# Attention and a cosine feed-forward layer on one core: cosine without an absolute value, weights' range by row sums, the state times r in 64x32 parts of the array, x's columns in another order

## The chip, the cores and the metric

The program runs on one core of a Trainium2 chip. The metric is its device time in microseconds, the median of several runs; lower is better. A profile of one execution stands beside the times.

## The reference

Two stages. A linear attention with a state per head (batch 4, 8 heads, 768 positions, 48 channels a head), and a feed-forward layer on its output (3072 tokens of 384 channels, 2048 hidden):

```python
for t in range(S):
    cur = einsum('bhd,bhe->bhde', u * k[t], v[t])
    y[t] = einsum('bhd,bhde->bhe', r[t], state + cur)
    state = w[..., None] * state + einsum('bhd,bhe->bhde', k[t], v[t])
x = y.transpose(0, 2, 1, 3).reshape(B * S, H * D)
h = x @ w_in
out = (h * cos(h)) @ w_out
```

The feed-forward weights `moe_w_in` and `moe_w_out` arrive as 64-bit floats; the others as 32-bit floats.

## The kernel before

**A written order.** Every operation (some instructions of one engine) is given to a planner (`Plan`, L72) with an engine, a due time, a cost and a latency in microseconds, what it comes after, and the buffers that it uses. The planner runs through a simulated clock, always starts the operation that can start first (among equals the one with the earlier due time), and gives buffers out of rings. What comes out is the program order of each engine; at run time each engine works through its instructions in that order, and waits where an input isn't there. The steps of the feed-forward part are the unit of due times. "ACT" is ScalarE, "DVE" VectorE, "POOL" GpSimd, "PE" TensorE, "SP" the engine that issues most DMAs.

**Attention** (`chunk`, L577) works on 24 chunks: 128 positions of one batch, all 8 heads, in four pairs of heads. A chunk loads r, k and v, brings k and r into transposed, decayed form (kT, rT), and forms the 128x128 scores A of each head on PE (`mm_a`, L736, 48 rows of the array, even heads in rows 0 to 47 and odd ones in 64 to 111, each half into its own PSUM bank). ACT writes the diagonal (`diagonal`, L726) and DVE puts the scores above it (`mask`, L745). The chunk's x, 384 rows of 128 positions in one PSUM bank, is the sum of two products: `mm_x` (L755), state times rT, in 12 matmuls with 112 rows and 32 columns of the array; and `mm_x2` (L765), v times A, in 16 matmuls with 128 rows and 32 columns. For `mm_x` the state `zc` of a batch, whose heads lie in two blocks of partitions, is first spread by two ACT copies into a tile `zt` that is zero elsewhere (`spread`, L786). x leaves PSUM once on ACT in rounded form (`xh`, L823) and once on DVE as the remainder (`xl`, L828). `mm_z` (L791) and `state` (L835) bring the state forward. Chunks 0 to 11 ("early") come before the feed-forward part and share seven PSUM banks; chunks 12 to 23 ("late") are woven into it, have three banks, and load r and k in pieces of 32 rows that DVE transposes.

**Weights.** 32 slices (16 of w_in, 16 of w_out, 384 KB each) are loaded into one of two `raw` buffers as pairs of 32-bit words (`load_raw`, L419), and turned into a high and a low part by `conv` (L485): ACT L511, DVE L519 and L531, POOL L542 (after which `raw` is free), ACT L547, DVE L552. Later every slice is loaded again and `check_range` (L429) tests that each value lies in the range in which that conversion is right: one ACT and four DVE instructions of 384 columns (L432, L438, L447, L456, L465). If any test fails, a flag makes the program run a slower general path behind the main one.

**The feed-forward part** has 128 steps: a slice of 128 hidden units for a block of three chunks. `mm_h` (L222) is nine matmuls of 384 columns into one of two or three PSUM banks; then come, in turn on ACT and DVE, `whole` (L241, h/2pi rounded to a whole number), `rest` (L244), `size` (L247, the absolute value), `cosine` (L250), the product with h (L944), and its high and low part (L947, L950); `mm_o` (L233) is nine matmuls into three accumulators. Blocks 0 to 3 go through slices 0-1, 2-4, 5-9 and 10-15 in turn, so the slices are needed one after another: slice 2 at step 8, slice 5 at step 20, slice 10 at step 40. An accumulator leaves through ACT (L978) or DVE (L980) and is stored by SP, or added in memory by a DMA of POOL.

Of the kernel before, what the change touches and what calls it, by code (L numbers as in the profile page):

```python
# [163 lines left out]
def kernel(  # L164
# [42 lines left out]
    quarter = const.tile([P, 1], F32, name="quarter")  # L207
    nc.vector.memset(quarter, 0.5 * math.pi)
# [32 lines left out]
    def whole(qi, ph):  # L241
        nc.scalar.activation(qi, ph, AF.Copy, scale=INV_2PI)  # L242
# [4 lines left out]
    def size(q):  # L247
        nc.scalar.activation(q, q, AF.Abs)  # L248

    def cosine(q):  # L250
        nc.scalar.activation(q, q, AF.Sin, scale=-TWO_PI, bias=quarter)  # L251


    with ExitStack() as actx:
# [12 lines left out]
        R_r = ring("r", 2, [P, H, DP], F32)  # L267
# [10 lines left out]
        R_f = ring("f", 8, [P, DM], F32)  # L278
# [21 lines left out]
        fine_all = att.tile([P, 2 * NF + 3], F32, name="fine")  # L300
        fine = fine_all[:, 0 : 2 * NF]
        fine_p = fine_all[:, 2 * NF : 2 * NF + 1]
        fine_m, fine_w = (fine_all[0:1, 2 * NF + i : 2 * NF + i + 1] for i in (1, 2))
# [14 lines left out]
        def start_pool2():  # L318
            for t in R_zt:
                nc.gpsimd.memset(t.ap, 0.0)  # L320
# [29 lines left out]
        b_w = Buf(B_EARLY)  # L350
        o_wT = op(PE, -95, 0.1, lambda: nc.tensor.transpose(b_w()[:, 0:NP], wr.rearrange("p j d -> p (j d)"), ident[0:NP, 0:NP]), [o_w, o_wr, o_pool], [b_w], lat=0.3)
# [67 lines left out]
        def load_raw(i, raw):  # L419
            f, part = divmod(i, 2)  # L420
            if part == 0:
# [7 lines left out]
        def check_range(i, due, behind):  # L429
            raw, ca, cb = Buf(R_raw), Buf(R_f), Buf(R_f)  # L430
            o0 = op(SP, due - 3.0, 1.6, lambda: load_raw(i, raw), [behind], [raw], lat=3.4)
            o1 = op(ACT, due, 0.47, lambda: nc.scalar.activation(ca(), f32(raw()[:, :, 1]), AF.Abs), [o0], [raw, ca])  # L432

            o2 = op(
                DVE,
                due,
                0.5,
                lambda: nc.vector.scalar_tensor_tensor(ca(), ca(), 0.0, ca(), op0=ALU.is_equal, op1=ALU.add),  # L438
                [o1],
                [ca],  # L440
                port=True,
            )
            o3 = op(
                DVE,
                due,
                0.27,
                lambda: nc.vector.tensor_scalar(cb(), ca(), F64_TINY, F64_HUGE, op0=ALU.max, op1=ALU.min),  # L447
                [o2],
                [ca, cb],
                port=True,  # L450
            )
            o4 = op(
                DVE,
                due,
                0.5,
                lambda: nc.vector.tensor_tensor(cb(), cb(), ca(), op=ALU.is_equal),  # L456
                [o3],
                [ca, cb],
                port=True,
            )  # L460
# [3 lines left out]
                0.5,  # L464
                lambda: nc.vector.tensor_reduce(fine[:, i : i + 1], cb(), op=ALU.min, axis=AX.X),  # L465
                [o4],
                [cb],
# [4 lines left out]
        def fine_min():  # L472
            nc.vector.tensor_reduce(fine_p, fine, op=ALU.min, axis=AX.X)
# [11 lines left out]
        def conv(i, due, behind=None):  # L485
# [20 lines left out]
            o0 = op(SP, due - 3.5, 1.6, lambda: load_raw(i, raw), [behind], [raw], lat=3.4)  # L506
# [54 lines left out]

        last_A = [None]
        last_z = [None] * B
# [13 lines left out]
        def chunk(i, due, xbuf):  # L577
# [11 lines left out]
            xp = Buf(bk)  # L589
# [11 lines left out]
            if late:  # L601
                rb = Buf(R_f)
                ks, rs = Buf(R_raw), Buf(R_raw)

# [39 lines left out]
            l_r = op(SP, due - 5.1, 1.35, load_r, ahead, [rb], lat=2.6, line=ln)  # L644
# [10 lines left out]
            if late:  # L655
# [10 lines left out]
                t_k = op(DVE, due - 2.9, 0.71, tr_s(kT, ks), [l_ks], [ks, kT])  # L666
                e_k = op(POOL, due - 2.8, 1.4, decay_s(kT, decT_k), [t_k], [kT], port=True)
                t_r = op(DVE, due - 2.8, 0.71, tr_s(rT, rs), [l_rs], [rs, rT])
                e_r = op(POOL, due - 2.7, 1.4, decay_s(rT, decT_r), [t_r], [rT], port=True)
            else:  # L670
                t_r = op(PE, due - 2.4, 0.43, tr(rTp, rb), [l_r, o_pool], [rb, rTp, rT], lat=0.3)
# [16 lines left out]
                [rb, kb, mb],  # L688
# [45 lines left out]
            o_d = [op(ACT, due - 1.55 + 0.01 * j, 0.9, diagonal(j), [o_a, o_pool], [ab, A[j]], line="diagonal") for j in range(2)]  # L734
# [17 lines left out]
            def xv():  # L752
                return xp()[:, 0 : NK * C].rearrange("q (kk t) -> q kk t", kk=NK)

            def mm_x():  # L755
                x = xv()
                for g in range(NK * 4):
                    p, s = divmod(g, 3)
                    gs = slice(G * (g % 4), G * (g % 4) + G)
                    nc.tensor.matmul(  # L760
                        x[gs, g // 4, :], zb()[:, p, G * s : G * s + G], rT()[0:KP, p, :], start=(g < 4), stop=False,
# [3 lines left out]
            def mm_x2():  # L765
                x = xv()
                for g in range(NK * 4):
                    p, s = divmod(g, 3)
# [30 lines left out]
            def mm_xz():  # L799
                if c:  # L800
                    mm_x()
# [360 lines left out]
```

## Time and profile before

| | |
|---|---|
| median of 3 runs | 528.02 us (526.63 to 528.57) |
| the profiled execution | 527.78 us, of which the span of the instructions is 526.1 us |
| PE busy | 511.6 us (97% of the span) |
| DVE, ACT, POOL busy | 427.2, 394.9, 177.4 us |
| granted TensorE clock, mean | 0.997 |
| DMA | 61.60 MB, mean 117 GB/s |

Busy time is that in which an engine has an instruction under way. Matmuls overlap, so PE's is not a measure of its work: for that, one reads when matmuls start. A group's row gives line, engine, operation, what it writes from what, shape and number, then busy us and mean ns of one, then idle time of the engine before these instructions and what ended it. PEld is PE's loading of weights into the array. SPq rows are DMAs that SP issues.

### The profile page before, as it was taken

The page shows a single profiled execution, that of the slowest core. Times are in us where ns is not written, and L with a number is a line of the kernel's source. Part 1 is how long each engine was busy: PE and PEld are TensorE (multiplying, and loading weights), DVE is VectorE, ACT ScalarE, POOL GpSimd, SP SyncE. Part 2 cuts the span into 40 slices and gives each one's busy share as a digit, 9 for nine tenths or more (in the row PEclk, how much of TensorE's full clock was granted, in tenths as well). Part 3 has the DMA queues.
Part 4 walks back from the last instruction along what each step waited for, and adds up shares of the span by engine and source line. Part 5 has one row for each costly group of instructions (what it writes and reads, how often), then busy time and mean ns, then how long its engine had stood idle before and what let it go on. Part 6 is the DMA issues. An engine that isn't in the chain of part 4 may idle for free.

```text
span 526.1 us, 11829 instructions
## 1 busy us (share of the span) xinstructions
PE 511.6 (97%) x4428; PEld 482.2 (92%) x4428; DVE 427.2 (81%) x835; ACT 394.9 (75%) x933; POOL 177.4 (34%) x184
## 2 busy tenths in 40 slices
PE   8999999999999999999999999899999999999995
PEld 6787799999999999999999999898999999999994
DVE  5688788889888787566899999999889998886453
ACT  3888988988888777758687787586867877776664
POOL 6766423255354244224426224404043040400000
PEclk9999999999999999999999999999999999999998
DMA  9897235667846495414584853646356453500001
GB/s 140 142 167 154 58 115 184 206 139 132 181 106 139 127 169 93 72 39 71 136 178 111 168 135 119 136 136 166 73 147 144 136 136 90 137 25 23 1 0 52
DMA packets 114979, 61.60 MB, mean 117 GB/s; under 512 B 78433, under 2 KB 110818, under 8 KB 114914
## 3 DMA queue, kind: packets, MB, share of 16 engines
q1 hardware_dynamic: 109586, 53.50, 42.2%
q0 software_dynamic: 5184, 7.08, 9.4%
q8 instruction: 36, 0.59, 0.5%
q14 instruction: 29, 0.24, 0.2%
q10 hardware_dynamic: 144, 0.20, 0.1%
HBM read 48.96 MB, written 11.80 MB: 115 GB/s over the span
## 4 chain that ended last, share of the span: by engine, by line
PE 70%; DVE 15%; ACT 8%; issue 3%; DMA 2%; POOL 1%; SPq 0%; DVEq 0%; ACTq 0%; POOLq 0%
PE bank L231 28%; PE bank L237 28%; PE bank L740 4%; PE bank L773 4%; DVE gl L950 3%; PE bank L760 2%; DVE f L944 2%; ACT A L730 2%; PE bank L651 2%; PE bank L795 1%; ACT gh L947 1%; DVE f L245 1%; DMA raw<-in_moe_w_out_dram 1%; DVE f L456 1%; ACT f L251 1%
## 5 line engine op out<-in xcount | busy, mean ns | idle before, releaser
L237 PE MATMUL bank<-w_out_hi,gl 128*128 128x384 f32 x384 | 130.7, 340 | 2.0 <-DVE gl L950 1.8
L231 PE MATMUL bank<-xh,w_in_hi 128*128 128x384 f32 x384 | 130.1, 339 | 2.1 <-DVE f L944 2.0
L237 PE MATMUL bank<-w_out_hi,gh 128*128 128x384 f32 x384 | 131.3, 342 | 0.7 <-ACT f L978 0.4
L237 PE MATMUL bank<-w_out_lo,gh 128*128 128x384 f32 x384 | 129.4, 337 | 0.0
L231 PE MATMUL bank<-xh,w_in_lo 128*128 128x384 f32 x384 | 129.4, 337 | 0.0
L231 PE MATMUL bank<-xl,w_in_hi 128*128 128x384 f32 x384 | 129.0, 336 | 0.0
L944 DVE TENSOR_TENSOR f<-bank,f 128x384 f32<-128x384 f32 (+1 forms) x132 | 71.4, 541 | 37.7 <-ACT f L251 37.1
L248 ACT ACTIVATE f<-f 128x384 f32<-128x384 f32 (+1 forms) x132 | 67.6, 514 | 39.9 <-DVE f L245 39.4
L950 DVE TENSOR_TENSOR gl<-f,gh 128x384 fp32r<-128x384 f32 (+1 forms) x132 | 85.1, 648 | 11.6 <-ACT gh L947 10.2
L947 ACT CAST gh<-f 128x384 fp32r<-128x384 f32 (+1 forms) x132 | 65.8, 500 | 31.6 <-DVE f L944 28.9
L245 DVE SCALAR_TENSOR_TENSOR f<-bank,qi 128x384 f32<-128x384 f32 (+1 forms) x132 | 70.7, 538 | 15.4 <-ACT qi L242 14.6
L242 ACT ACTIVATE qi<-bank 128x384 int32<-128x384 f32 (+1 forms) x132 | 62.1, 474 | 27.0 <-PE bank L231 26.9
L251 ACT ACTIVATE f<-f,quarter 128x384 f32<-128x384 f32 (+1 forms) x132 | 79.7, 605 | 2.2
L231 PEld LDWEIGHTS bank<-xh,w_in_hi 128*128 128x128 f32 x384 | 72.1, 188 | 4.9 <-DVE f L944 2.1
L237 PEld LDWEIGHTS bank<-w_out_hi,gl 128*128 128x128 f32 x384 | 72.0, 188 | 4.3 <-DVE gl L950 3.8
L237 PEld LDWEIGHTS bank<-w_out_hi,gh 128*128 128x128 f32 x384 | 72.0, 187 | 3.9 <-ACT f L978 1.2
L231 PEld LDWEIGHTS bank<-xl,w_in_hi 128*128 128x128 f32 x384 | 72.1, 188 | 0.2 <-DVE xl L828 0.2
L231 PEld LDWEIGHTS bank<-xh,w_in_lo 128*128 128x128 f32 x384 | 72.1, 188 | 0.0
L237 PEld LDWEIGHTS bank<-w_out_lo,gh 128*128 128x128 f32 x384 | 72.0, 188 | 0.0
L730 ACT ACTIVATE A<-ident,a 128x128 f32<-128x128 f32 x192 | 59.7, 391 | 6.3 <-DVE a L721 6.1
L664 POOL TENSOR_TENSOR kT<-kT,decT_k 112x512 f32<-112x512 f32 x12 | 16.3, 1357 | 134.7 <-DVE kT L659 99.4
L542 POOL TENSOR_TENSOR f<-f,raw 128x384 int32<-128x384 int32 x32 | 38.8, 1212 | 65.4 <-DVE f L531 22.5
(88 smaller groups left out, 678.8 us busy)
## 6 DMA issues: line engine op xcount, KB each, us to landing
raw<-in_moe_w_in_dram SPq DMA_DIRECT2D x32, 384.0 KB, 3.3
raw<-in_moe_w_out_dram SPq DMA_DIRECT2D x32, 384.0 KB, 3.2
out_dram<-f POOLq DMA_DIRECT2D x36, 192.0 KB, 5.3
k<-in_k_dram SPq DMA_DIRECT2D x24, 192.0 KB, 3.6
v<-in_v_dram SPq DMA_DIRECT2D x24, 192.0 KB, 4.2
raw<-in_k_dram SPq DMA_DIRECT2D x47, 96.0 KB, 2.4
raw<-in_r_dram SPq DMA_DIRECT2D x47, 96.0 KB, 2.3
out_dram<-f SPq DMA_DIRECT2D x23, 192.0 KB, 3.1
```

The costliest lines, as they stand in the source:

```text
L231: nc.tensor.matmul(ph, a, b_, start=(i == 0), stop=(i == len(mm) - 1))
L237: nc.tensor.matmul(acc, a[:, ts], b_[:, f, :], start=(first and i == 0), stop=(last and i == 2))
L242: nc.scalar.activation(qi, ph, AF.Copy, scale=INV_2PI)
L245: nc.vector.scalar_tensor_tensor(q, ph, INV_2PI, qi, op0=ALU.mult, op1=ALU.subtract)
L248: nc.scalar.activation(q, q, AF.Abs)
L251: nc.scalar.activation(q, q, AF.Sin, scale=-TWO_PI, bias=quarter)
L542: lambda: nc.gpsimd.tensor_tensor(ai(), ai(), cn(), op=ALU.add),
L730: nc.scalar.activation(A[j]()[:, p, :], ident, AF.Copy, scale=ab()[:, h : h + 1])
L740: nc.tensor.matmul(cube(Ap[j])[:, p, :], kT()[ps, p, :], rT()[ps, p, :], start=True, stop=True)
L944: nc.vector.tensor_tensor(g()[:, cs], ph()[:, cs], q()[:, cs], op=ALU.mult)
L947: nc.scalar.copy(gh()[:, cs], g()[:, cs])
L950: nc.vector.tensor_tensor(gl()[:, cs], g()[:, cs], f32(gh())[:, cs], op=ALU.subtract)
```

## The change

- `whole` adds 0.25 before rounding and `cosine` takes the sine of 2pi q + pi/2 with the constant in the instruction; the absolute value between them goes.
- `check_range` lets the ACT instruction also sum the absolute values of each row, and one DVE instruction sum those below the lower limit; the two sums are compared with the limits once at the end (`fine_min`). Three DVE instructions of a slice go.
- The state is no longer spread. State times rT is made of 16 matmuls with 48 rows and 32 columns (parts of 64x32 of the array), straight from `zc`, whose heads are now padded to 64 columns with zeros; even heads write one PSUM bank and odd ones another. v times A goes into the same two banks, still 16 matmuls.
- So x's 384 rows come out in another order (`x_columns`), and in three pieces: three ACT copies and three DVE subtractions instead of one each. w_in's rows are loaded in the same new order: a slice takes eight DMAs instead of one.
- The seven early banks are written once at the start (`start_banks`), since the pieces read places that nothing else has written.
- A third `raw` buffer, in the place of the early chunks' r tiles, and a ninth buffer `f`.
- Some of the planner's costs are others.

```diff
     def whole(qi, ph):
-        nc.scalar.activation(qi, ph, AF.Copy, scale=INV_2PI)
+        nc.scalar.activation(qi, ph, AF.Copy, scale=INV_2PI, bias=0.25)
...
-    def size(q):
-        nc.scalar.activation(q, q, AF.Abs)
-
     def cosine(q):
-        nc.scalar.activation(q, q, AF.Sin, scale=-TWO_PI, bias=quarter)
+        nc.scalar.activation(q, q, AF.Sin, scale=TWO_PI, bias=0.5 * math.pi)
...
+        r_all = att.tile([P, 2, H, DP], F32, name="r_all")
+        R_r = [Tile(r_all[:, i]) for i in range(2)]
+        raw_r = Tile(r_all.rearrange("q i h d -> q (i h d)")[:, 0 : 2 * DM].bitcast(I32).rearrange("q (f w) -> q f w", w=2))
...
-        R_f = ring("f", 8, [P, DM], F32)
+        R_f = ring("f", 9, [P, DM], F32)
...
-        R_raw = ring("raw", 2, [P, DM, 2], I32)
+        R_raw = ring("raw", 2, [P, DM, 2], I32) + [raw_r]
...
-        zc = [att.tile([KP, NP, D], F32, name=f"zc{b}") for b in range(B)]
-        R_zt = ring("zt", 2, [KP, NP, 2 * D], F32)
+        zc = [att.tile([KP, NP, DP], F32, name=f"zc{b}") for b in range(B)]
...
+        def start_banks():
+            for b_ in b_0:
+                nc.tensor.matmul(
+                    b_().rearrange("q (a t) -> q a t", a=4),
+                    warm,
+                    warm[:, None, :].to_broadcast([P, 4, P]),
+                    start=True,
+                    stop=True,
+                )
...
-        def load_raw(i, raw):
+        def load_raw(i, raw, by_x=False):
             f, part = divmod(i, 2)
-            if part == 0:
+            if part == 0 and by_x:
+                rl = 2 * DFF
+                for kk in range(NK):
+                    g = 0
+                    while g < 4:
+                        first = x_columns(kk, g)
+                        n = 2 - len(first) + 1
+                        (h0, skip0), (h1, skip1) = (x for i in range(n) for _, x in x_columns(kk, g + i))
+                        c0, c1 = h0 * D + max(skip0, 0), h1 * D + max(skip1, 0)
+                        nc.sync.dma_start(
+                            raw()[32 * g : 32 * (g + n)].rearrange("p (kk f) w -> p kk (f w)", kk=NK)[:, kk],
+                            bass.AP(
+                                tensor=w_in_w.tensor,
+                                offset=w_in_w.offset + c0 * rl + f * P * 2,
+                                ap=[[(c1 - c0) * rl, 2], [rl, 16 * n], [1, 2 * P]],
+                            ),
+                        )
+                        g += n
+            elif part == 0:
...
         def check_range(i, due, behind):
...
+                lambda: nc.scalar.activation(
+                    ca(), f32(raw()[:, :, 1]), AF.Abs, accum_out=fine[:, i : i + 1]
+                ),
...
+                lambda: nc.vector.scalar_tensor_tensor(
+                    cb(), ca(), F64_TINY, ca(), op0=ALU.is_lt, op1=ALU.mult,
+                    accum_out=fine[:, 2 * NF + i : 2 * NF + i + 1],
+                ),
...
+        def x_columns(kk, g):
+            j, m, which = (
+                ((0, 0, 0), (0, 0, 1), (0, 0, 2), (0, 1, 2)),
+                ((0, 1, 0), (0, 1, 1), (1, 0, 0), (1, 0, 1)),
+                ((1, 0, 2), (1, 1, 2), (1, 1, 0), (1, 1, 1)),
+            )[kk][g]
+            one, two = 4 * m + j, 4 * m + j + 2
+            return (((0, (one, 0)),), ((0, (two, 16)),), ((0, (one, 32)), (16, (two, -16))))[which]
...
-            o0 = op(SP, due - 3.5, 1.6, lambda: load_raw(i, raw), [behind], [raw], lat=3.4)
+            o0 = op(SP, due - 3.5, 1.6 if part else 2.7, lambda: load_raw(i, raw, True), [behind], [raw], lat=3.4)
...
             def mm_x():
...
+                if c:
+                    for n, (h, skip, i, at, g) in enumerate(PARTS):
+                        p, j = divmod(h, 2)
+                        ps = slice(j * DP, j * DP + D)
+                        e0 = p * DP + skip
+                        nc.tensor.matmul(
+                            xv(i)[G * g : G * g + G, at, :],
+                            zc[b].rearrange("q p e -> q (p e)")[ps, e0 : e0 + G],
+                            rT()[ps, p, :],
+                            start=(n < 8), stop=False, skip_group_check=True,
+                        )
+                for n, (h, skip, i, at, g) in enumerate(PARTS):
...
+                        vb().rearrange("q h d -> q (h d)")[:, e0 : e0 + G],
+                        A[j]()[:, p, :],
...
+            def x_parts():
+                top = slice(P // 2, P)
+                return (
+                    (slice(0, P), slice(0, 2), xv(0)),
+                    (top, slice(1, 2), xv(1)[top, 0:1]),
+                    (slice(0, P), slice(2, 3), xv(1)[:, 1:2]),
+                )
...
-                o3 = op(ACT, dd + 0.7, 0.44 * one, f_size, [o2], [q], line="size", lat=0.1)
-                o4 = op(ACT, dd + 0.8, 0.44 * one, f_cos, [o3], [q], line="cos")
+                o4 = op(ACT, dd + 0.8, 0.52 * one, f_cos, [o2], [q], line="cos")
```

`PARTS` lists the 16 parts so that eight in a row are eight different parts of the array (two halves of rows, four of columns).

More of the change, by code (lines that the diff above doesn't have):

```diff
@@ L299 @@
         warm = att.tile([P, P], BF16, name="warm")
[L300 to L303, printed above, removed]
+        fine_all = att.tile([P, 4 * NF + 3], F32, name="fine")
+        fine = fine_all[:, 0 : 4 * NF]
+        fine_p = fine_all[:, 4 * NF : 4 * NF + 1]
+        fine_m, fine_w = (fine_all[0:1, 4 * NF + i : 4 * NF + i + 1] for i in (1, 2))
         plan = Plan()
@@ L431, in check_range @@
             o0 = op(SP, due - 3.0, 1.6, lambda: load_raw(i, raw), [behind], [raw], lat=3.4)
-            o1 = op(ACT, due, 0.47, lambda: nc.scalar.activation(ca(), f32(raw()[:, :, 1]), AF.Abs), [o0], [raw, ca])
-            o2 = op(
-                DVE,
-                due,
[L437 to L459, printed above, removed]
+            o1 = op(
+                ACT,
+                due,
+                0.55,
+                lambda: nc.scalar.activation(
+                    ca(), f32(raw()[:, :, 1]), AF.Abs, accum_out=fine[:, i : i + 1]
+                ),
+                [o0],
+                [raw, ca],
             )
@@ L557, in conv @@
             return o8
+        PARTS = []
+        for t in range(2):
+            for j in range(2):
+                for g in range(4):
+                    some = [(*x, j, kk - j, g) for kk in range(NK) for _, x in x_columns(kk, g) if x[0] % 2 == j]
+                    PARTS.append(some[t])
         last_A = [None]
+        r_first = Buf([raw_r])
         last_z = [None] * B
@@ L588, in chunk @@
             A = [Buf(R_A) for _ in range(2)]
-            xp = Buf(bk)
+            xp = [Buf(bk) for _ in range(2)]
             zp = Buf(bk)
@@ L603, in chunk @@
                 ks, rs = Buf(R_raw), Buf(R_raw)
+            rbs = [rb] if late else [rb, r_first]
             def rn():
@@ L687, in chunk @@
                 [l_r, l_k],
-                [rb, kb, mb],
+                [*rbs, kb, mb],
                 port=True,
@@ L732, in diagonal @@
                 return go
-            o_d = [op(ACT, due - 1.55 + 0.01 * j, 0.9, diagonal(j), [o_a, o_pool], [ab, A[j]], line="diagonal") for j in range(2)]
+            o_d = [op(ACT, due - 1.55 + 0.01 * j, 1.18, diagonal(j), [o_a, o_pool], [ab, A[j]], line="diagonal") for j in range(2)]
             def mm_a():
@@ L782, in chunk @@
-            zb = Buf(R_zt)
-            o_zt = []
-            if c:
-                def spread(j):
-                    ps = slice(j * DP, j * DP + D)
-                    return lambda: nc.scalar.copy(zb()[ps, :, j * D : (j + 1) * D], zc[b][ps])
-                o_zt = [op(ACT, due - 1.9, 0.25, spread(j), [last_z[b], o_pool2], [zb]) for j in range(2)]
             def mm_z():
@@ L846, in chunk @@
                 last_z[b] = op(
-                    DVE, due + 1.4, 0.3 if c == 0 else 0.65, state, [zo, *o_zt, last_z[b], o_pow], [zp]
+                    DVE, due + 1.4, 0.3 if c == 0 else 0.65, state, [zo, xo, last_z[b], o_pow, o_pool2], [zp]
                 )
```

114 lines of the change are left out of this document (52 added, 62 removed).

## The prediction

> **What bounds the kernel now.** I read the page first, then a table of stages (a stretch, its length, then busy time of PE, PEld, DVE, ACT and POOL, clock, DMA share, GB/s), with bounds at the first matmul of the feed-forward part and at PE's end.
>
> ```profile
> span 526.1 us, 11829 instructions
> ```
>
> ```profile
> 0.00:64.40 64.40, 60.65 (x1076) 47.91 (x1076) 48.14 (x103) 48.23 (x141) 41.56 (x56) 1.00 0.75 134
> 64.40:180.00 115.60, 114.45 (x694) 111.73 (x692) 99.26 (x205) 99.11 (x225) 46.54 (x46) 1.00 0.62 149
> ...
> 300.00:410.00 110.00, 106.87 (x928) 101.07 (x928) 102.02 (x185) 80.62 (x186) 35.48 (x30) 1.00 0.52 130
> 410.00:520.20 110.20, 110.12 (x789) 106.35 (x787) 82.07 (x172) 79.92 (x186) 11.51 (x12) 1.00 0.25 65
> ```
>
> The first 64.4 us are attention for 12 chunks, with no engine alone in charge. From there PE sets the time: 455.8 us. The chain of waits gives one step of the feed-forward part:
>
> ```profile
> 144.82 1.57 PE bank L231 x9
> 146.40 1.58 PE bank L237 x9
> ```
>
> A step is 3.15 us, so 128 steps are 403 us. The twelve late chunks stand between them:
>
> ```profile
> 224.19 1.16 PE L740 MATMUL bank<-rT,kT 48*128 48x128 f32 x16
> 225.28 0.44 PE L237 MATMUL bank<-w_out_hi,gh 128*128 128x384 f32 x1
> 228.62 0.86 PE L760 MATMUL bank<-rT,zt 112*32 112x128 f32 x24
> 229.30 1.08 PE L773 MATMUL bank<-A,v 128*32 128x128 f32 x32
> 230.31 0.56 PE L795 MATMUL bank<-v,k 128*48 128x48 f32 x16
> 230.81 0.45 PE L237 MATMUL bank<-w_out_hi,gh 128*128 128x384 f32 x1
> ```
>
> By starts one takes 1.09 + 2.19 us, and 0.1 us more before and after each of its two blocks: 12 x 3.3 is 40 us, so some 13 us of 455.8 are stalls. Those that the list of waits names are mostly DVE's, and DVE is busiest (102 of 110 us) in 300 to 410:
>
> ```profile
> PEld bank L237 <- DVE gl L950: 3.8, 7, 1.2
> PEld bank L231 <- DVE f L944: 2.1, 4, 0.7
> SPq L422 <- POOL f L542: 41.4, 13, 10.5
> SPq L427 <- POOL f L542: 40.5, 14, 5.1
> ```
>
> The last two rows are the weight loads: each waits until POOL gives one of two raw buffers back.
>
> **The change part by part: what gets cheaper.** The groups that go or stay (busy time and ns of one stand behind the bar):
>
> ```profile
> L248 ACT ACTIVATE f<-f 128x384 f32<-128x384 f32 (+1 forms) x132 | 67.6, 514 | 39.9 <-DVE f L245 39.4
> L788 ACT COPY zt<-zc 48x192 f32<-48x192 f32 x40 | 13.9, 348 | 1.4 <-PE bank L760 1.1
> L438 DVE SCALAR_TENSOR_TENSOR f<-f 128x384 f32<-128x384 f32 x32 | 18.0, 564 | 0.6 <-ACT f L432 0.6
> L447 DVE TENSOR_SCALAR f<-f 128x384 f32<-128x384 f32 x32 | 11.2, 352 | 0.1
> L456 DVE TENSOR_TENSOR f<-f,f 128x384 f32<-128x384 f32 x32 | 20.3, 635 | 0.1
> L465 DVE TENSOR_REDUCE fine<-f 128x1 f32<-128x384 f32 x32 | 17.2, 540 | 0.1
> ```
>
> The absolute value takes 67.6 us off ACT, the spread of the state 13.9. A range check keeps one DVE instruction of some 0.56 us out of four: 66.7 - 18 = 49 us off DVE, nearly all between 230 and 490 us. What the accumulating forms add is unseen: between nothing and a second small instruction each (0.27 us, by the pieces quoted below), at most 9 us on each engine, beside what is saved. All this is off PE's path and pays only through stalls: from 0 to -13 us. I take **-6**: the two DVE rows.
>
> **State matmuls.** Now 24 instructions (two passes of 12) on four column parts take 229.30 - 228.62 = 0.68 us, so 0.11 us a round of four. The new form has 16 matmuls, 32 instructions, on eight parts. L740's halves already run side by side into two banks (16 in 1.09 us, where one part at 0.11 us each would need 1.8). So four rounds of eight, 0.44 us. But 64-row parts and the 128-row matmuls with v behind them are two shapes, and a change of shape costs 0.1 to 0.2 us by the rows above (from 225.28 the next matmul starts 0.28 us later instead of 0.18). 0.44 + 0.15 against 0.68 is -0.09 a chunk: **-1 us** over the 12 late ones; without a switch -2.9; if the row halves didn't overlap (0.88) +4.
>
> [...]
>
> **x in three pieces.** Two more copies on ACT and two more subtractions on DVE for each chunk. Small pieces at the end of the run price them:
>
> ```profile
> 517.83 0.81 ACT L947 CAST gh<-f 128x128 fp32r<-128x128 f32 x3
> 518.16 0.79 DVE L950 TENSOR_TENSOR gl<-f,gh 128x128 fp32r<-128x128 f32 x3
> ```
>
> So 0.27 us a piece and some +0.35 us a chunk on each engine. Late it hides under PE. In the first 64.4 us ACT gains 0.35 (two spreads of 0.35 go), DVE loses 0.35 of 4, and x holds two of seven PSUM banks instead of one: -3 to +5 us, taken as 0. The seven matmuls that fill the banks take the place of warm-up matmuls, which wait for nothing either.
>
> **The weight loads** decide. A w_in slice was one transfer; it becomes eight, each with two runs of 16 or 32 rows as its outermost count. Today:
>
> ```profile
> 74.31 0.38 SPq L422 DMA_DIRECT2D raw<-in_moe_w_in_dram  x1
> 174.26 0.38 SPq L422 DMA_DIRECT2D raw<-in_moe_w_in_dram  x1
> ```
>
> ```profile
> raw<-in_moe_w_in_dram SPq DMA_DIRECT2D x32, 384.0 KB, 3.3
> raw<-in_r_dram SPq DMA_DIRECT2D x1, 23.2 KB
> ```
>
> Twelve pairs (w_in and w_out) in 99.95 us: 8.33 us a pair, landing 3.3 us after issue. Issue costs 8 x 0.38 = 3.0 us of SP, which mostly waits. The question is how many of the 16 DMA engines move a piece. The trace has one load with an odd outermost count, the piece of 31 rows in the last chunk (`part(3, 0, 31, ...)`, 23.2 KB). It is alone on the queue for a moment; the other rows are a whole w_in slice and loads in pieces of 32 rows (DMA share and GB/s stand last):
>
> ```profile
> 445.30:447.00 1.70, 1.70 (x12) 1.70 (x11) 1.58 (x5) 0.49 (x1) 0.00 (x0) 1.00 0.65 160
> 447.46:447.53 0.07, 0.07 (x2) 0.07 (x2) 0.07 (x1) 0.07 (x1) 0.00 (x0) 1.00 0.06 22
> 75.36:77.19 1.83, 1.83 (x11) 1.65 (x11) 1.66 (x4) 1.79 (x4) 0.00 (x0) 1.00 0.73 214
> ```
>
> 0.06 is one engine of 16, at 22 GB/s. So the outermost count decides: 31 goes to one engine, 32 and 128 to all. A count of 2 should go to two. Bounds: 16 engines, 1.8 us of data as now; two engines, 196.6 KB each at 22 KB/us, **8.9 us**. I take two, by the 31-row load.
>
> [...]
>
> If always the same two engines serve, a pair costs them 8.9 us, 1.1 for their share of w_out (24.6 KB) and 0.5 for a store: 10.5 us. How much PE work lies between two pairs is fixed by program order, and the planner that makes it still reckons with 3.4 us behind a start of 2.7. Bounds: as now, 8.33 us; with three raw buffers instead of two, 8.33 x 2/3 = 5.6. Between them DVE decides:
>
> ```profile
> L245 DVE SCALAR_TENSOR_TENSOR f<-bank,qi 128x384 f32<-128x384 f32 (+1 forms) x132 | 70.7, 538 | 15.4 <-ACT qi L242 14.6
> L944 DVE TENSOR_TENSOR f<-bank,f 128x384 f32<-128x384 f32 (+1 forms) x132 | 71.4, 541 | 37.7 <-ACT f L251 37.1
> L950 DVE TENSOR_TENSOR gl<-f,gh 128x384 fp32r<-128x384 f32 (+1 forms) x132 | 85.1, 648 | 11.6 <-ACT gh L947 10.2
> L519 DVE TENSOR_SCALAR f<-raw 128x384 int32<-128x384 int32 x32 | 12.8, 400 | 2.3 <-DMA raw<-in_moe_w_out_dram 2.3
> L531 DVE SCALAR_TENSOR_TENSOR f<-raw,f 128x384 int32<-128x384 int32 x32 | 17.7, 552 | 0.4
> L552 DVE TENSOR_TENSOR w_out_lo<-f,w_out_hi 128x384 fp32r<-128x384 f32 x16 | 9.6, 602 | 0.3 <-ACT w_out_hi L547 0.3
> ```
>
> A step uses 1.73 of 3.15 us, a pair needs 2 x 1.55: 2.2 steps, 6.8 us. When a load is late, ACT's conversion (L511) and DVE's L519 wait for it, and behind them in the same queues stand whole, rest, cosine and gate of the running steps; their PSUM banks fill and PE stops. So 10.5 - 6.8 = 3.7 us a pair, for 13 of the 14 pairs after the first units (one is fetched ahead): **+48 us**, from 29 (8.33) to 64 (5.6). In the early stage the first w_in slice stands ahead of k, r and v on those two engines; there POOL already waits for k:
>
> ```profile
> 32.22 1.33 SPq L422 DMA_DIRECT2D raw<-in_moe_w_in_dram  x1
> 35.36 1.01 POOL L686 TENSOR_TENSOR f<-r,k 128x384 f32<-128x384 f32 x1 [1.87 <-DMA k<-in_k_dram]
> ```
>
> A slice from 32.2 ends near 42, two us after k would have landed: +2 (0 to 5).
>
> **Sum.** 526.1 - 6 - 1 + 48 + 2 = 569.1 us of span. The profiled run took 527.78, 1.7 more than its span, and stands 0.24 below the median 528.02: **571 us**, +8%. Its own range, by the bounds: 545 to 592.
>
> **Rivals.** (a) *The pieces go over all engines*, or land soon enough; then the first paragraphs hold alone: 526.1 - 6 - 1 with 0 to 2 for eight issues instead of one, 521 with what lies around the span (514 to 528). For it: pieces of 32 rows do use all (0.65); against it: the 31-row load. It decides if a slice still lands within some 6 us. (b) *Narrow loads, but placed by need*: if program order held the conversions back to their due step, pairs of 10.5 us from 63 us on would bring the tenth slice at 147 and have it converted near 151, where step 24 needs it at 140, and the sixteenth in time: +11 instead of +48, 534. Against it: today's pairs run as soon as POOL frees a buffer (41.4 and 40.5 us of waits). (c) *Spread loads, but DVE and the banks rule the early stage*: +0.35 us for 12 chunks and a bank's wait of 0.5 each, +10, less 7: 531. (d) The flag comes out as 0 and the general path runs: milliseconds; the sums of 384 values near 1 are far from the limit.
>
> **Chances.** Forecast 0.67, (a) 0.24, (b) 0.04, (c) 0.04, (d) 0.01. A measurement of this kernel can tell 0.5%, 2.6 us. Faster: most of (a), 0.22; same, the rest of (a) and the low ends of (b) and (c), 0.05; slower 0.73. The range leaves out the faster half of (a) and the top of the forecast: 519 to 592.
>
> **What would show it.** Two engines: DMA share near 0.13 while a w_in slice lands, 9 to 11 us from its first issue; ACT and DVE waiting for raw in 64 to 210; PE's 128 steps slower there only; w_in loads ending past 200 us instead of 174. Gains: no stall beyond 1 us in 300 to 410, DVE near 80 of 110 us; state and v matmuls in 1.6 us. I am wrong if a slice lands in 6 us or less, or if PE stays over 95% busy in 64 to 180.

## The result and the profile after

The changed kernel takes **588.86 us** (median of 4 runs, 585.59 to 592.48). The kernel before, run beside it, takes 527.4 us. The ratio is 1.116, with a 95% interval from 1.113 to 1.120: 61 us slower. The forecast was 571 us, slower; the time lies in its range, near the upper end.

The profiled execution took 585.59 us. The span, and the table of stages with the columns of the prediction's (the last row is a stretch that the kernel before didn't have):

```profile
span 583.8 us, 12485 instructions
```

```profile
0.00:64.40 64.40, 56.01 (x950) 43.42 (x952) 46.51 (x108) 40.25 (x125) 38.05 (x54) 0.97 0.75 128
64.40:180.00 115.60, 89.41 (x642) 83.50 (x638) 72.23 (x151) 57.64 (x140) 35.39 (x33) 0.87 0.41 111
180.00:217.00 37.00, 29.38 (x135) 28.23 (x136) 24.70 (x51) 20.37 (x46) 12.84 (x13) 0.84 0.43 100
217.00:300.00 83.00, 80.28 (x521) 78.89 (x521) 52.23 (x96) 43.34 (x95) 23.37 (x24) 0.97 0.43 81
300.00:410.00 110.00, 109.06 (x1010) 102.78 (x1009) 86.47 (x170) 67.26 (x178) 38.84 (x36) 1.00 0.59 133
410.00:520.20 110.20, 110.20 (x1025) 104.32 (x1024) 82.83 (x170) 69.81 (x189) 29.96 (x27) 1.00 0.51 128
520.20:576.30 56.10, 56.09 (x322) 55.67 (x320) 33.24 (x79) 28.57 (x69) 0.00 (x0) 1.00 0.04 12
```

PE, which was busy for 114.45 of 115.60 us in the second row before, is now busy for 89.41, at a mean granted clock of 0.87. From 300 us on it is as dense as before. PE ends at 576.3 us instead of 520.2, so the loss lies in the first 230 us.

The list of waits names what the engines wait for there (engine, line, what ended it: us in all, times, longest). L548 and L556 are ACT's and DVE's first instruction on a raw slice; `raw` and `r_all` are the raw buffers:

```profile
ACT raw L548 <- DMA raw<-in_moe_w_in_dram: 30.0, 6, 8.3
ACT r_all L548 <- DMA r_all<-in_moe_w_in_dram: 23.5, 6, 6.2
DVE f L556 <- DMA raw<-in_moe_w_in_dram: 19.7, 5, 6.2
DVE f L556 <- DMA r_all<-in_moe_w_in_dram: 18.3, 5, 5.8
```

None of these four stood among the longest waits before. The loads themselves, in the order of time (start, us from the first to the last issue of the eight, engine and line). Before, each was one issue of 0.38 us, and the last began at 174.26:

```profile
64.03 5.32 SPq L442 DMA_DIRECT2D r_all<-in_moe_w_in_dram  x8
...
106.70 6.81 SPq L442 DMA_DIRECT2D r_all<-in_moe_w_in_dram  x8
117.58 6.79 SPq L442 DMA_DIRECT2D raw<-in_moe_w_in_dram  x8
...
209.53 7.28 SPq L442 DMA_DIRECT2D r_all<-in_moe_w_in_dram  x8
```

From 64.03 to 209.53 are 13 pairs in 145.5 us: 11.19 us a pair instead of 8.33.

One stall seen from close by. The slice issued at 106.70 has landed when ACT's L548 goes on at 120.59, 13.9 us later. In ACT's queue the rounding of w_out, `gh` and the copy of an accumulator (L1023) stand behind L548, and PE stands still until that copy:

```profile
116.15 0.34 SPq L457 DMA_DIRECT2D raw<-in_moe_w_out_dram  x1
117.58 6.79 SPq L442 DMA_DIRECT2D raw<-in_moe_w_in_dram  x8
120.59 0.54 ACT L548 ACTIVATE r_all<-r_all 128x384 int32<-128x384 uint32 x1 [6.19 <-DMA r_all<-in_moe_w_in_dram]
...
122.78 0.69 PE L235 MATMUL bank<-w_out_hi,gh 128*128 128x384 f32 x1 [6.61 <-ACT f L1023]
```

The table of stages for the same time, cut at the stall's ends, and beside it a stretch inside it in which hardly anything else moves (the last three columns are granted clock, DMA share of 16 engines, GB/s):

```profile
115.84:122.78 6.94, 0.33 (x2) 0.01 (x1) 1.39 (x5) 2.19 (x6) 0.00 (x0) 0.80 0.47 146
122.78:126.70 3.92, 3.92 (x12) 3.92 (x13) 3.92 (x10) 2.51 (x6) 1.21 (x1) 0.50 0.25 92
126.70:130.00 3.30, 3.30 (x20) 3.30 (x20) 1.64 (x4) 1.01 (x2) 1.23 (x1) 0.97 0.84 256
```

```profile
120.00:125.00 5.00, 2.22 (x7) 2.22 (x8) 3.44 (x8) 4.02 (x10) 1.08 (x1) 0.50 0.13 49
```

Two things are to be read here. The share of 0.13 is two engines of 16 (0.125), though several of a slice's eight pieces are in flight: all of them go to the same two. And after 6.94 us without work PE runs for 3.92 us at half its clock: only 12 matmuls, where the next 3.30 us hold 20.

### The profile page after: what moved, and what is told of

Same layout as the page of the kernel before. It is cut to its first block, busy times and chain, and to the rows that moved or that the text cites. A ratio compares the mean times of both kernels' runs of the same rounds, so it can differ in the third digit from the quotient of the medians.

```text
span 583.8 us, 12485 instructions
## 1 busy us (share of the span) xinstructions
PE 530.4 (91%) x4593; PEld 496.8 (85%) x4593; DVE 398.3 (68%) x820; ACT 327.7 (56%) x841; POOL 178.4 (31%) x186
## 4 chain that ended last, share of the span: by engine, by line
PE 64%; DMA 17%; DVE 6%; SPq 6%; ACT 3%; issue 1%; POOL 1%; DVEq 0%; POOLq 0%; ACTq 0%
PE bank L235 28%; PE bank L229 26%; DMA raw<-in_moe_w_in_dram 8%; SPq L442 6%; DMA r_all<-in_moe_w_in_dram 5%; PE bank L791 3%; PE bank L823 3%; DMA r_all<-in_moe_w_out_dram 2%; PE bank L812 2%; DMA k<-in_k_dram 1%; ACT A L781 1%; DVE A L797 1%; PE bank L836 1%; DVE xl L876 1%; DVE rT L727 1%
## 5 line engine op out<-in xcount | busy, mean ns | idle before, releaser
L235 PE MATMUL bank<-w_out_hi,gh 128*128 128x384 f32 x384 | 135.7, 353 | 16.1 <-ACT f L1023 13.0
L229 PE MATMUL bank<-xh,w_in_hi 128*128 128x384 f32 x384 | 133.6, 348 | 10.7 <-DVE f L990 10.7
L235 PE MATMUL bank<-w_out_hi,gl 128*128 128x384 f32 x384 | 134.3, 350 | 8.2 <-DVE gl L996 8.2
L235 PE MATMUL bank<-w_out_lo,gh 128*128 128x384 f32 x384 | 133.5, 348 | 0.0
L229 PE MATMUL bank<-xh,w_in_lo 128*128 128x384 f32 x384 | 132.7, 346 | 0.0
L229 PE MATMUL bank<-xl,w_in_hi 128*128 128x384 f32 x384 | 132.6, 345 | 0.0
L996 DVE TENSOR_TENSOR gl<-f,gh 128x384 fp32r<-128x384 f32 (+1 forms) x132 | 80.1, 609 | 31.5 <-ACT gh L993 31.2
L229 PEld LDWEIGHTS bank<-xh,w_in_hi 128*128 128x128 f32 x384 | 75.4, 196 | 12.7 <-DVE f L990 11.6
L579 POOL TENSOR_TENSOR f<-f,raw 128x384 int32<-128x384 int32 x22 | 25.4, 1153 | 72.2 <-DVE f L568 23.4
L797 DVE COPY_PREDICATED A<-upper,bank 128x512 f32<-128x512 int32 x48 | 34.6, 739 | 16.6 <-PE bank L791 11.8
```

The source lines that it names most:

```text
L229: nc.tensor.matmul(ph, a, b_, start=(i == 0), stop=(i == len(mm) - 1))
L235: nc.tensor.matmul(acc, a[:, ts], b_[:, f, :], start=(first and i == 0), stop=(last and i == 2))
L579: lambda: nc.gpsimd.tensor_tensor(ai(), ai(), cn(), op=ALU.add),
L797: return lambda: nc.vector.copy_predicated(A[j](), upper[:, None, :].to_broadcast([P, NP, C]), cube(Ap[j]))
L996: nc.vector.tensor_tensor(gl()[:, cs], g()[:, cs], f32(gh())[:, cs], op=ALU.subtract)
```

## The experiments

The first theory was the prediction's: pieces with an outermost count of 2 are moved by two engines, and since the order of the work is fixed, the conversions wait and PE with them. The rivals were the number of transfers, the new x and its banks, and the rest of the change.

**One transfer a slice again.** PE, DVE, ACT and POOL have the same instructions in the same order as in the changed kernel.

```diff
-            o0 = op(SP, ..., lambda: load_raw(i, raw, True), [behind], [raw], lat=3.4)
+            o0 = op(SP, ..., lambda: load_raw(i, raw), [behind], [raw], lat=3.4)
```

> The changed kernel with each w_in slice loaded by one transfer again, as before; everything else, the planner's figures and the order of the work on PE, DVE, ACT and POOL among it, is as changed. What it leaves out: w_in's rows are not brought into x's new order. Theory (two of 16 DMA engines carry the eight pieces, and the running order waits for them): all the loss goes, the median is 521 us (514 to 528), a slice lands within 4 us, ACT and DVE no longer wait for raw between 64 and 210 us, and the granted clock is 1.00 again. Rival (x in three pieces and the two banks rule the early stage, where the changed kernel was some 13 us late): the first 77 us stay as long as changed and the median is 530 to 540. Rival (the rest of the change is what costs): over 560.

Measured: 528.17 us; against the kernel before 1.000 (0.998 to 1.003; numbers given so are the ratio and its 95% interval). The narrow loads cost 588.86 - 528.17 = **60.7 us**, which is all of the loss. The same stretch of the program, from the second step's first matmul to the thirty-first's, in the changed kernel, and then with one transfer (same columns):

```profile
77.10:217.10 140.00, 108.69 (x517) 104.38 (x514) 86.18 (x178) 68.65 (x158) 43.10 (x41) 0.85 0.42 107
```

```profile
71.60:164.10 92.50, 91.78 (x518) 90.76 (x515) 86.69 (x176) 68.14 (x157) 43.30 (x41) 0.98 0.66 169
```

The same matmuls take 47.5 us longer: 30.6 us in which PE is idle, and 16.9 us more of busy time, at a clock of 0.85. Ahead of the stretch lie 5.5 us (77.1 against 71.6), behind it 5.4 more up to the thirty-fourth step; from there to PE's end the distance between the two kernels stays at 58.4 us.

But the time didn't come to 521: without the narrow loads the rest of the change gains nothing. The runs further down take that apart.

**The same rows in twelve transfers with outermost counts of 32 and 16.** Pairs of blocks of 32 rows that lie in the same partitions go together; blocks of two runs of 16 rows are cut in two.

```diff
-                                ap=[[(c1 - c0) * rl, 2], [rl, 16 * n], [1, 2 * P]],
+                    ap = [[rl, n], [more * rl, 2], [1, 2 * P]] if more else [[rl, n], [1, 2 * P]]
...
+                for g, k0 in ((0, 0), (1, 0), (2, 1), (3, 1)):
+                    ...
+                    piece(32 * g, 32, k0, c0, c1 - c0)
+                for g, kk in ((2, 0), (3, 0), (0, 2), (1, 2)):
+                    for at, (h, skip) in x_columns(kk, g):
+                        piece(32 * g + at, 16, kk, h * D + max(skip, 0))
```

> The changed kernel with the same rows to the same places, but each w_in slice cut into twelve transfers whose outermost count is 32 or 16 instead of eight whose outermost count is 2; order and the planner's figures as changed. Theory (outermost count decides how many engines serve): every piece goes over 16 engines, a slice lands within some 6 us of its first issue (twelve issues of 0.38 us are 4.6 us), and the median is 521 to 528. Rival (it is the number of transfers: SP spent 5 to 9.5 us to issue eight): twelve cost half as much again, 7 to 14 us a slice, and the median is 590 to 640.

Measured: 543.41 us, 1.028 of the time before (1.024 to 1.032): 45 us better than the change, with half as many transfers more; 15 us worse than one transfer, so outside both expected ranges. The issues, and the stretch that took 140.0 and 92.5 us:

```profile
115.81 5.89 SPq L438 DMA_DIRECT2D raw<-in_moe_w_in_dram  x12
...
142.64 5.45 SPq L438 DMA_DIRECT2D raw<-in_moe_w_in_dram  x12
```

```profile
75.70:181.40 105.70, 95.04 (x517) 90.81 (x514) 87.07 (x176) 68.76 (x158) 43.22 (x41) 0.97 0.61 146
```

Each issue takes SP 0.42 us, twelve of them 5.45 us, and where the trace shows the landing of a whole slice in this stretch, it comes 6.7 to 9.5 us after the first issue. The rival's mechanism is real, but small: +13.2 us in the stretch against +47.5.

**Eight transfers of 48 KB, with an outermost count of 16.** As many as the change's, whose pieces are of 32 or 64 KB (48 on average); 16 partitions each, in runs of 1 KB as there.

```diff
+                for g in range(8):
+                    nc.sync.dma_start(
+                        raw()[16 * g : 16 * g + 16].rearrange("p (kk f) w -> p kk (f w)", kk=NK),
+                        w_in_w[:, ...].rearrange("(kk p) f -> p kk f", p=P)[16 * g : 16 * g + 16],
```

> The changed kernel with each w_in slice in eight transfers of 48 KB as changed, but each with an outermost count of 16 (16 partitions, three blocks of 1 KB each) instead of 2. What it leaves out: w_in's rows are not brought into x's order. Theory (the count of 2 is what costs, the number of transfers only through SP: eight issues of 0.45 us, 3.6 us, a slice landing within 6 us): 528 to 536, between one transfer (528) and twelve (543). Rival (eight transfers a slice are slow in themselves): 570 to 590.

Measured: 531.00 us, 1.005 of the time before (1.003 to 1.008). The stretch:

```profile
75.10:168.60 93.50, 91.47 (x518) 89.17 (x515) 86.94 (x176) 68.23 (x157) 43.17 (x41) 1.00 0.68 164
```

93.5 against 92.5 and 140.0 us. With the number of transfers and their mean size held, the outermost count makes the difference between 531 and 589 us; the twelve transfers, which bring the change's own rows to the change's own places, rule out that the order of the rows does. Ahead of the stretch it is otherwise: it starts at 75.1 us here, 75.7 with twelve transfers and 77.1 in the change, against 71.6 with one. Of the change's 5.5 early us, 3.5 come with eight wide transfers too. By engines, the runs show two counts: 2 at a share of 0.13, which is two of 16, and in the kernel before the 31 rows at 0.06, one. For 16 there is only the mean of the stretch with all its transfers, 0.68 at 164 GB/s, against 0.42 at 107 in the change. And the shares of 0.65 and 0.73, which the prediction has for 32 and 128, are 10 to 12 engines on the mean; that it is all 16 was the author's estimate.

**The narrow pieces alone, in the kernel before.**

```diff
-            o0 = op(SP, due - 3.5, 1.6, lambda: load_raw(i, raw), ...
+            o0 = op(SP, due - 3.5, 1.6, lambda: load_raw(i, raw, True), ...
```

> The kernel before with each w_in slice loaded by the changed kernel's eight pieces of outermost count 2, nothing else changed (order of the work on PE, DVE, ACT and POOL as before). What it leaves out: x's columns are not put in the order of the rows that these pieces bring, so the product is of other rows. Theory: this part alone costs most of the loss. A pair takes the two engines 10.5 to 11.5 us where PE has 8.33 us of work, so 13 pairs lose 28 to 41 us; with two raw buffers a slice can't be fetched ahead of the conversion before it, which may add some 2 us a pair: 556 to 595. Rival (the narrow loads cost only in the changed order or with the rest of the change): 528 to 535.

Measured: 645.2 us (one run), 50 more than the highest that was expected. The table of stages between two loads, and SP's longest wait:

```profile
103.62:118.33 14.71, 11.32 (x56) 11.01 (x55) 7.11 (x16) 7.10 (x16) 2.26 (x2) 0.85 0.30 95
```

```profile
SPq L441 <- POOL f L571: 108.3, 14, 13.2
```

A pair takes 14.7 us here, and 14.0 to 18.9 elsewhere (13 pairs from 73.21 to 283.77 us, 16.2 on average): with two raw buffers a slice can be asked for only when POOL has given its buffer back, so landing and conversion add up instead of overlapping.

**The changed kernel with two raw buffers** tests that.

```diff
-        R_raw = ring("raw", 2, [P, DM, 2], I32) + [raw_r]
+        R_raw = ring("raw", 2, [P, DM, 2], I32)
```

> The changed kernel with two raw buffers instead of three, narrow loads as changed. Theory (the narrow loads in the kernel before took 14.7 us and more a pair, since a slice could be asked for only when a buffer came back, and the third buffer is what brings that to 11): 610 to 645. Rival (the third buffer does nothing; the kernel before took 645 for another reason): 582 to 596.

Measured: 614.5 us (one run). A pair takes 15.1 us again (13 from 73.34 to 269.80 us), where the change with its third buffer takes 11.19. So the third buffer hides 26 us of the narrow loads.

**The planner told of the slow loads.**

```diff
-            o0 = op(SP, due - 3.5, 1.6 if part else 2.7, ..., lat=3.4)
+            o0 = op(SP, due - 3.5, 1.6 if part else 6.8, ..., lat=3.4 if part else 6.0)
```

> The changed kernel with the same eight narrow pieces, but the planner that writes out the order is told 6.8 us of SP and 6.0 us to landing for a w_in slice instead of 2.7 and 3.4. Theory (the loss is less the engine time than the order, which puts conversions ahead of the running steps before their data is there): the conversions stand later, the steps in between go on, and the median is 534 to 555, with ACT's and DVE's waits for raw less than half of the changed kernel's 53 and 38 us. Rival (the two engines' 10.5 us a pair set the time whatever the order): 575 to 590.

Measured: 566.1 us (one run), between the two ranges. The w_in loads stand no closer (61.89 to 212.20 us, 13 pairs of 11.6 us), but more steps lie between two conversions: the 29 steps from the second to the thirty-first take 110.6 us, 9.6 pairs, where the change has 12.5. So some 23 us of the 60.7 come from the order that didn't know, and the rest wasn't to be had by these two figures.

**New cosine and new range check alone, in the kernel before.** This and the next four take up why the rest of the change gained nothing.

```diff
-        nc.scalar.activation(q, q, AF.Sin, scale=-TWO_PI, bias=quarter)
+        nc.scalar.activation(q, q, AF.Sin, scale=TWO_PI, bias=0.5 * math.pi)
...
+                    ca(), f32(raw()[:, :, 1]), AF.Abs, accum_out=fine[:, i : i + 1]
```

> The kernel before with the new cosine and the new range check and nothing else of the change; the 268 bytes of the sums lie in the place of the w tile, which is used up by then. With one transfer a slice the changed kernel stood at 528, not at 521: its first matmul of the steady feed-forward steps was 7 us late (71.6 instead of 64.4 us) and what followed was 9.5 us shorter. Theory (these two edits relieve ACT and DVE after 64 us, and the early lateness comes from x's part): the first step starts at 64 to 65 us and the median is 519 to 523. Rival (the relief is not theirs, or the early stage is late through the new order that the planner writes once ACT's and DVE's prices change): 526 to 530.

Measured: **522.76 us, 0.990 of the time before (0.985 to 0.994)**, the fastest kernel of all. The chain that ended last, by engine, and the stage in which the prediction looked for the gain:

```profile
PE 94%; DVE 2%; ACT 1%; issue 1%; ACTq 0%
```

```profile
300.00:410.00 110.00, 110.00 (x954) 105.66 (x953) 80.31 (x161) 70.44 (x186) 34.09 (x30) 1.00 0.53 138
```

PE has 94% of that chain (before: 70%, with 15% for DVE), and no idle time is left from 300 to 410 us (before: 3.1 us).

**The range check alone.** The last line of that diff without the cosine:

```diff
+                    ca(), f32(raw()[:, :, 1]), AF.Abs, accum_out=fine[:, i : i + 1]
...
+                    op0=ALU.is_lt,
+                    op1=ALU.mult,
+                    accum_out=fine[:, 2 * NF + i : 2 * NF + i + 1],
```

> The kernel before with the new range check alone (the sums in the place of the w tile). With the new cosine beside it, it took 522.8 us, and PE had no stall behind 64 us. Theory (the prediction's: the 49 us off DVE, nearly all in the late chunks, are what relieves PE): 521 to 524 us, and PE busy over 109 of 110 us from 300 to 410. Rival (it is the cosine: 67.6 us off ACT, and one step less in the chain from PE's result to the gate): 526 to 529.

Measured: 526.66 us, 0.999 (0.998 to 1.000): no gain by the time. Yet the trace has the relief: PE was busy for 109.58 us from 300 to 410, and it ended earlier. The last pieces of the chain, in this kernel, in the kernel before, and with cosine and range check:

```profile
510.61 5.16 PE bank L237 x27
```

```profile
515.01 5.17 PE bank L237 x27
```

```profile
507.77 4.78 PE bank L235 x27
```

PE ended 4.4 us before the kernel before's, and with the cosine too 7.6 us. What lies behind PE's end grew in return: 9.2 us with the range check alone and 8.0 with both, against 5.9 before (last section). These are figures of one execution each. The cosine alone was not run.

**x's part alone, in the kernel before** (state product, two banks, three pieces, new order; w_in in one transfer):

```diff
-            xp = Buf(bk)
+            xp = [Buf(bk) for _ in range(2)]
...
+                            zc[b].rearrange("q p e -> q (p e)")[ps, e0 : e0 + G],
+                            rT()[ps, p, :],
...
+                for rows, kk, src in x_parts():
+                    nc.scalar.copy(xbuf()[0][rows, kk], src)
```

> The kernel before with the new state product, the two banks, x in three pieces and x's new order, and nothing else; w_in is loaded by one transfer as before. What it leaves out: w_in's rows are not brought into x's order. Theory (x's part makes the early stage late: three pieces on ACT and DVE and a seventh bank a chunk): the first steady step starts at 70 to 73 us and the median is 532 to 536 (7 us later, 1 us less in the late chunks). Rival (the early lateness is the third raw buffer's or the planner's, which are not in here): 526 to 529.

Measured: 537.27 us, 1.018 (1.013 to 1.024), more than expected.

Where the steady steps start has to be counted alike. In the kernel before, the first block of `mm_h` runs at 64.4 us, ahead of the last early chunk's x, and the second starts at 67.8, when all early chunks are done. The other kernels bring the first block further forward (to 62.9 us here, 48.3 with one transfer, 51.9 in the change), and the 70.2 us expected and measured here are those of the second. Against 67.8 that is 2.4 us late, not 6; stalls in the next blocks make it 5.7. In the late part it loses again: it is 3.8 us behind after 120 of the 256 blocks of `mm_h` and `mm_o`, 7.5 after 140, and PE ends 5.8 us later. Its stage from 300 to 410 us:

```profile
300.00:410.00 110.00, 106.97 (x1037) 99.13 (x1036) 101.99 (x198) 80.17 (x188) 30.81 (x26) 1.00 0.54 129
```

**x in one piece, banks held as long**, on top of one transfer a slice:

```diff
-                for rows, kk, src in x_parts():
-                    nc.scalar.copy(xbuf()[0][rows, kk], src)
+                nc.scalar.copy(xbuf()[0], xv3())
```

> The changed kernel with each w_in slice loaded by one transfer, and with x copied and subtracted in one piece each from the first of the two banks; both banks are held as long as before, and the order is the same. What it leaves out: w_in's rows are not brought into x's order, and what stands in the second bank is not read, so x is not the reference's. Theory A (the pieces make the early stage late: 0.35 us more a chunk on ACT and on DVE, with the chain through them): the first steady step starts at 64 to 67 us and the median is 519 to 523. Theory B (the banks make it: seven a chunk of seven there are instead of six): it starts at 70 to 72 us and the median is 526 to 529.

Measured: 526.40 us, 0.996 (0.994 to 0.999). The pieces cost 528.17 - 526.40 = 1.8 us, little beyond the two intervals; the second block of `mm_h` stays at 71.7 us. So the pieces aren't what makes the early stage late.

**An idle seventh bank, in the kernel before:**

```diff
-            xp = Buf(bk)
+            xp, xq = Buf(bk), Buf(bk)
```

> The kernel before with one more PSUM bank held by each chunk, from the matmuls that write x until x's low half is read, as the change holds two; nothing is put into it. The planner, which knows of the bank, writes its order with it. Theory (banks make the early stage late: seven instead of six for each chunk, and seven there are): the first steady step starts at 69 to 72 us instead of 64.4 and the median is 532 to 537. Rival (the lateness comes of the state, which is read by PE itself in the change and can't be brought forward before that): 526 to 529.

Measured: 534.54 us, 1.014 (1.011 to 1.016). The time is the expected one, the place only in part: the first block of `mm_h` starts at 65.4 us (before: 64.4), the second at 69.4 (before: 67.8). So 1.6 us are lost early, of the 2.4 that x's part alone loses by then and the 3.8 of the change with one transfer. At the sixty-first step the kernel stands 1.1 us ahead of before, at the seventy-first 6.4 us behind, and PE ends 5.1 us later. Those steps lie among the late chunks, which have three banks, not seven. So a second bank a chunk has most of its price there; what makes the rest of the early lateness isn't shown.

**The change without x's part and without the narrow loads** (cosine, range check, third raw buffer, the planner's new prices; the last two beside the diff of cosine and range check):

```diff
+        R_raw = ring("raw", 2, [P, DM, 2], I32) + [raw_r]
...
-                t_k = op(DVE, due - 2.9, 0.71, tr_s(kT, ks), [l_ks], [ks, kT])
+                t_k = op(DVE, due - 2.9, 0.95, tr_s(kT, ks), [l_ks], [ks, kT])
...
-            o_d = [op(ACT, due - 1.55 + 0.01 * j, 0.9, ...
+            o_d = [op(ACT, due - 1.55 + 0.01 * j, 1.18, ...
```

> The changed kernel without x's part and without the narrow loads: new cosine, new range check, the third raw buffer in r's place and the planner's new prices; eight f buffers as before. Theory (a third buffer and the prices do nothing where a slice lands in 3.3 us): 520 to 524, as with cosine and range check alone (522.8). Rival (the buffer in r's place makes the early loads of r wait for conversions, or the prices make a worse order): 525 to 529.

Measured: 529.98 us, 1.006 (1.004 to 1.008): 7.2 us more than with cosine and range check alone. Its first stages, and then those of cosine and range check alone:

```profile
0.00:64.00 64.00, 61.96 (x1068) 49.57 (x1069) 50.15 (x101) 48.38 (x142) 42.31 (x56) 1.00 0.76 141
64.00:77.00 13.00, 9.29 (x106) 8.67 (x103) 11.50 (x25) 8.68 (x22) 4.64 (x4) 0.87 0.42 124
77.00:180.00 103.00, 99.90 (x567) 98.36 (x565) 97.74 (x184) 72.77 (x166) 49.84 (x49) 1.00 0.72 173
```

```profile
0.00:64.00 64.00, 60.42 (x1065) 47.95 (x1067) 47.72 (x101) 47.86 (x140) 41.79 (x56) 1.00 0.74 135
64.00:77.00 13.00, 13.00 (x134) 12.50 (x133) 12.49 (x26) 10.63 (x26) 3.11 (x3) 1.00 0.41 124
77.00:180.00 103.00, 103.00 (x591) 102.90 (x590) 88.94 (x182) 75.01 (x169) 43.27 (x44) 1.00 0.62 154
```

The first three w_in slices are asked for at 23.08, 45.98 and 56.01 us instead of 32.2, 52.7 and some 64; the third of them goes into the new buffer. Conversions move forward into a time in which DVE has little left: it is busy for 97.74 of 103 us up to 180 us (88.94 without), and PE loses 3.7 and 3.1 us in the second and third row. The 3.7 are one stall, up to 69.96 us, that ends with ACT's rounding of a w_in slice (L541). Which of the buffer and the prices the planner's order owes this to wasn't separated.

## Why the prediction was right, and where not

Right in direction and mechanism; 571 against 588.9 us. The terms by themselves:

- **Weight loads, +48** (29 to 64): right, as a term. Two engines serve (share 0.13), the waits are ACT's and DVE's for raw, PE is busy for 77% from 64 to 180 us, the last load starts at 209.53, and nothing is lost behind the thirty-fourth step. Between one transfer and the change lie 52.9 us from the second step to there, the stretch of the prediction's thirteen pairs. The parts of the product were less good than it: a pair took 11.19 us, not 10.5, and had 91.8 / (140.0 / 11.19) = 7.3 us of PE's work, not 6.8; 3.9 us a pair came out beside the forecast 3.7. That two misses cancel is luck. And the prediction had all of it as idle time. PE was idle for 30.6 of the 47.5 us; the other 16.9 were busy time at a lower clock (0.85 in the stretch, 0.98 with one transfer). In the stall from 115.84 to 122.78 the granted clock is still 1.00 from 118.00 to 119.90 and 0.50 from 120.05 on, and the first 3.92 us of work behind it have 0.50. Behind a shorter stall it was the same: after 2.69 us with next to no matmuls (97.00 to 99.69) the next 3.01 us ran at 0.50.
- **Landing**: 9 to 11 us from the first issue were forecast. The first two slices, with no other w_in slice in flight, took 11.2 and 10.6 us to their last packet; with a third buffer a slice can be issued while the one before it is still moving (that of 96.11 up to 109.0 us), and the one quoted, issued at 106.70, took 13.3 us (ACT went on after 13.9).
- **Early stage, +2** (0 to 5): mis-sized. The second block of `mm_h` starts at 77.1 instead of 67.8 us. 5.5 us of these 9.3 go with the eight loads of a slice (3.5 are there with wide ones, so some 2 are left for the two engines); the other 3.8 are there with one transfer.
- **Stall relief, -6**: PE ended 7.6 us earlier with cosine and range check alone, and the time was 4.4 us less, so the size was good. That it all was the two DVE rows' isn't: range check alone, the time gains nothing measurable, and 4.4 us by PE's end. The cosine has a share. The 13 us of stalls that the term was to come from were too many: 12 x 3.3 leaves out the 0.1 us before and after each block (with them it is 44, and 9 us of stalls), and PE was idle for 4.8 us from 64.4 to 520.2.
- **State matmuls, -1**: as worked out. State and v matmuls together took 1.60 us in a late chunk (0.60 for 32 instructions, then 1.01), where 0.44 + 0.15 + 1.01 was forecast.
- **What failed** has no line in the sum: **the third raw buffer and the planner's new prices were costed at nothing** where a slice lands in time. They are +7.2 us. **x in three pieces, 0** (-3 to +5), holds only in company: alone, x's part is +10 us; on top of the kernel without it (and with a ninth f buffer) it is 528.17 - 529.98, some 2 us less (3 by the ratios, since the two ran beside different runs of the kernel before). So -4.4 (cosine and range check), +7.2 and -1.8 end at 528.2, the time before. Forecast for the same was 526.1 - 6 - 1 + 1.7, 521. These 7 us, together with some 10 us more for the narrow loads than +48 and +2, are the 18 by which the forecast was short.

Of the rivals, (a) said 521 with wide loads: the eight wide transfers took 531 and one took 528, so it too was short by 7 to 10 us. (b), order by need at 534, is what the run with the planner told came nearest to, and that took 566: the order alone returns a good third. (c), banks and DVE in the early stage, at +10, was too high: the lateness there is 3.8 us with one transfer, of which an idle bank alone makes 1.6 and the pieces nothing.

What stays open: whether it is the third buffer or the prices that write the early conversions too early; what makes the rest of the early lateness; and why x's part costs 10 us alone and nothing with cosine and range check beside it. DVE, busy for 102 of 110 us in the late stage there and for 80 to 85 with the new range check, is a likely reason, but it was only argued.

## What to carry to other kernels

When a load is cut up to bring its rows into another order, look at the outermost count of each piece first: eight pieces of 48 KB with a count of 16 cost 3 us here, eight of 48 KB on average with a count of 2 cost 61 us. Where the order of the work is written ahead, a transfer's true time belongs in the planner, and every buffer and price that comes with a change is an edit of its own: here they ate the gain of the parts that were good. Leave the other parts away and cosine and range check alone make the kernel 1% faster.

## What the runs showed of the hardware

**An issue takes longer in a slice that is asked for while an earlier one is in flight.** With two engines serving, the sixth of a slice's eight issues mostly took SP 1.2 to 2.3 us instead of 0.62 from the fifth slice on, and all eight then took 6.6 to 9.6 us: 1.66 us in the slice of 106.70, 2.3 us ahead of the last packet of the one before, but 0.62 in that of 199.66, 1.3 us ahead; the w_out load and the stores of SP stand behind them. With two raw buffers, where pairs stand 15.1 us apart, the eight mostly take 4.95 us (and 4.96 at 103.62 us in the run with the narrow pieces alone). What holds SP up isn't shown.

**The last packets of the program are instructions.** What lies behind PE's end differs from kernel to kernel (5.9 to 9.2 us) though the last stores are the same. The DMA records from the stores' last packet to the end, before, and then with cosine and range check (40 equal slices; then what moved):

```profile
DMA  5009000400000000000400000000000000000000
...
q14 instruction: 3, 0.02, 3.6%
q8 instruction: 1, 0.02, 2.6%
```

```profile
DMA  0600000040000100000000000000000010000000
...
q14 instruction: 4, 0.03, 2.1%
q8 instruction: 1, 0.02, 1.7%
```

The windows are 523.9 to 526.1 and 515.6 to 520.6 us, so a slice is 0.055 and 0.125 us. No data moves any more, only instructions. The last packet starts at 525.0 in the one and at 519.7 in the other, 0.7 and 2.4 us after the packet ahead of it, and the program ends some 1 us behind each. If the end waits for the last of them, 2 to 3 us hang on when it comes; range check alone, with 9.2 us behind PE's end, lost 3.3 of its 4.4 us there. Whether it waits isn't shown.
